# Layer 2's second weight: loaded and converted late, by halves with their own scales, and its output summed in two banks

## The chip, the cores and the metric

The kernel runs on one core of one Trainium2 chip. The metric is device time in microseconds for one execution; shown is the median over runs. Five engines work side by side, each with its own queue that it works through in order: TensorE (PE, matmuls, with its weight loads as PEld), VectorE (DVE), ScalarE (ACT), GpSimd (POOL) and SyncE (SP, which issues the DMAs). In this kernel TensorE's results go to PSUM tiles (three called pb of 1024 fp32 columns, g2_ps and xn_ps of 512); the other tiles lie in SBUF, and two tensors of intermediate results in DRAM.

## The reference

Attention over two sequences of 768 tokens with 8 heads of 64, in which a query sees only the keys whose cluster (the nearest of 16 centroids) is its own; then two feed-forward layers on the 1536 tokens:

```python
x = attn_out.transpose(0, 2, 1, 3).reshape(1536, 512)
h = x @ moe_w_in;   g = h * cos(h);                  x = g @ moe_w_out     # layer 1: 512 -> 2048 -> 512
h = x @ moe2_w_in;  g = h * (1 / (1 + exp(-h)));     out = g @ moe2_w_out  # layer 2: 512 -> 2048 -> 512
```

The four feed-forward weights arrive as fp64 and are read as pairs of 32-bit words, which the kernel puts together into fp32 on the chip ("conversion"); the rest is fp32, and so is the output.

## The kernel before, in words

**Precision.** Each matmul operand is held as two fp16 tiles, a high part and a low part, after multiplication by a power of two, its scale; a product is three matmuls (high x high, high x low, low x high). A scale needs a bound of the whole tensor: the sum of squares of the converted weight, per partition by ScalarE (L438), then over partitions by a small matmul with ones (`all_sum`, L422), then four single-column instructions on VectorE (L443 to L447).

**Order.** The kernel writes down tasks with an engine (sometimes two to choose from), a duration, dependencies, buffers and a priority; a planner (`Graph.run`) simulates them as a list schedule (the ready task with the smallest priority number goes first on its engine) and the instructions are issued in the order that comes out. So each engine's order is fixed in advance by the planner's own durations, and a queue waits where the chip is later than the plan. Work of unit u (128 or 256 tokens) has priority about 1000 x u, layer 2 has `base` = 100000, and the late numbers in `T` shift groups of tasks against each other.

**Stages.** Layer 1's weights are converted first. Seven units of attention follow, each with its scores, softmax, transposes of the probabilities (by DMA, L514) and product with the values (L958); layer 1 of a unit is interleaved with the next unit's attention (L1034 to L1036 into h, L1092 to L1094 out of g). When the last attention task is done, the SBUF tiles of attention are given up and layer 2's are laid in their place (the task `SWAP`).

**Second weight of layer 2, before.** `w2_convert` (L868) has priority 1e6, the last of all, and runs during attention. For each of 16 blocks of 128 x 512 it loads 512 KB of raw words (L692), converts them with VectorE (L704, L706, and L716 in three of four blocks; the fourth has its low word added by ScalarE L710 and GpSimd L711) into half of the tile x2s, takes the squares (L438) and stores 256 KB to DRAM (L875). The swap waits for it. In layer 2 it comes back in 8 loads of 512 KB into two buffers `st` (L1162) and is split (`split`, L752): high part by GpSimd (L754) or ScalarE (L753), rescaling in place by ScalarE (L498), low part by VectorE (L500). Its scale is made to match the two halves of the first weight, so that all 16 blocks of the inner dimension add up in one bank.

**First weight of layer 2.** After the swap, 16 loads into two buffers `ws2`, each converted by VectorE through a PSUM bank (L698, L701, L713), with a scale for each half (inner blocks 0 to 7 and 8 to 15), and split into l2["w"][0] and [1] (L753, L754, L765); the converted fp32 values lie where the second weight's fp16 parts go later, l2["w"][2] and [3].

**Layer 2's passes.** 512 tokens at a time, three times: load x2 from DRAM, maximum over all (L430, L431), scale, split (L1197 ScalarE, L1199 VectorE); 16 blocks of 12 matmuls each into three banks pb (L1217 to L1219), each followed by ScalarE (L1231, L1235) and VectorE (L1233, L1237) that form g; then 4 output blocks of 48 matmuls (L1252 to L1254) into the banks g2_ps and xn_ps in turn, copied out by ScalarE with the factor (L1258) and stored (L1261). "Pass" below is 192 matmuls: an in-pass and an out-pass for each of three groups of tokens, six in all.

Of the kernel before, what the change touches and what calls it, by code (L numbers as in the profile page):

```python
# [22 lines left out]
         PREP=-1178, PREPQ=1263, LD=-4837, LOB=-0.79, WB=-1, HB=1, EB=5, KB=-1.47, GB=1.71, CB=0.8, XB=-0.2, SB=0.71,  # L23
# [229 lines left out]
def mm(n, count):  # L253
    return 0.025 + count * n / 2400.0
# [6 lines left out]
def dma(nbytes):  # L261
    return max(0.18, nbytes / 360e3)
# [9 lines left out]
def fused_kernel(tc, q, k, v, cent, w1i, w1o, w2i, w2o, out, dbg=None):  # L272
# [4 lines left out]
    P = 128  # L277
# [24 lines left out]
    with tc.manual_schedule(), tc.tile_pool(name="dram", bufs=1, space=DRAM) as dpool:  # L302
        x2_dram = dpool.tile([P, ND, B * S], F32, name="x2_dram")
        w2_dram = dpool.tile([P, ND * DF], F32, name="w2_dram")
# [63 lines left out]
        p_x2s, p_w2s = BufPool([x2s[:, :WC]]), BufPool([x2s[:, WC:]])  # L368
# [496 lines left out]
        w2_done = []  # L865
        w2_mx = col(NW)

        def w2_convert():  # L868

            for i in range(NW):  # L870
                fb = Buf(p_w2s)
                pr = 1e6 + i * 10
                t, tq = conv(lambda fb=fb: fb.ap, w2_mx[:, i:i + 1], w2o[i * P:(i + 1) * P, :].bitcast(I32), 0, pr, fb, dst_deps=x_free if 2 in WX else (), add_low=i % 4 < LOW[2], via=i % 4 < VIA[2])
                w2_done.append(tq)
                w2_done.append(add("SP", dma(P * WC * 4), lambda i=i, fb=fb: SP.dma_start(  # L875
                    out=w2_dram[:, i * WC:(i + 1) * WC], in_=fb.ap), [t], pr - 3, use=[fb], lat=SLAT))

# [184 lines left out]
        x2max, x2done = {}, {}  # L1062

        def layer1_out(u):
# [15 lines left out]
            for dp in range(ND // 2):  # L1080
# [28 lines left out]
                te[2 * i:2 * i + 2], pr, use=[x2b[i]], lat=SLAT) for i in range(2)]  # L1109
            x2done[u] = [tmx, *tds]  # L1110
# [5 lines left out]
        def layer2(l1_last):  # L1116
            base = 1e5
            t_swap = add("SWAP", 0.01, lambda: None, [*attn_tasks, *w2_done], 0)
            l2["swap"] = t_swap

            s, inv = [col() for _ in range(3)], [col() for _ in range(3)]
            ready = {}
            mx0 = col(NW)
            p_ws2 = BufPool([0, 1], fifo=False)
            raw = lambda r: l2["w"][:, 2:4].rearrange("p a b -> p (a b)").bitcast(F32)[:, r]
            ms = [[], []]
            for n in range(NW):
                i = (n % 8) // 2 * 4 + n // 8 * 2 + n % 2
                r = slice(i * WC, (i + 1) * WC)
                ms[n // 8] += conv(lambda r=r: raw(r), mx0[:, n:n + 1], w_in_src(w2i, i), 0, base + n * 10 - T["W2"], None, p_ws2, [t_swap], add_low=n % 4 < LOW[3], via=n % 4 < VIA[3])  # L1130
# [206 lines left out]
```

## Time and profile before

| | |
|---|---|
| median of 3 runs | 808.01 us (806.83 to 808.8) |
| profiled execution | 810.0 us, of which the span from first to last instruction 807.2 |
| busy, share of the span | TensorE 711.8 us (88%), VectorE 546.0 (68%), ScalarE 491.0 (61%), GpSimd 287.8 (36%) |
| mean granted TensorE clock | 0.979 of full speed |
| DMA traffic | 111.29 MB, mean 138 GB/s |
| second weight's transfers | 16 of 24 loads of 512 KB (median 4.8 us to landing), 16 stores of 256 KB (2.9), 8 loads of 512 KB (3.9) |

Busy time is a share over stages with different limits: in the attention stage several engines are near their limit, in layer 2 TensorE alone. The profile lists, for each group of instructions of one line, the busy time, the mean of one and the idle time of its engine in front of them with what ended it; waits are put down to the event that came last.

### The profile page before, as it was taken

Reading aid. Unit: us, or ns where it says so; the run is one execution under the profiler, and the core shown is the slowest. Engines: PE = TensorE matmul, PEld = TensorE weight load, DVE = VectorE, ACT = ScalarE, POOL = GpSimd, SP = SyncE. Lnnn points to the kernel's source line nnn. Section 1 sums busy time; section 2 is a strip of 40 time slices with the busy share of each in tenths; the row PEclk is TensorE's granted clock in tenths of the full one; section 3 lists DMA queues with packets and bytes.
Section 4 is the critical chain, followed back from the end, with each engine's and each line's share of the span. In section 5 each row is a group of like instructions: output and inputs, shape, how many; then the busy total and the mean of one; then the engine's idle time right before and its main releaser. Section 6 shows DMA issues by size and latency. Waiting matters only on the chain.

```text
span 807.2 us, 16855 instructions
## 1 busy us (share of the span) xinstructions
PE 711.8 (88%) x6745; PEld 483.9 (60%) x6745; DVE 546.0 (68%) x1156; ACT 491.0 (61%) x769; POOL 287.8 (36%) x240
## 2 busy tenths in 40 slices
PE   2468777988969998998999999998999899999998
PEld 1344344867757876876887888883444344444443
DVE  7899798998987899697688764878850355005400
ACT  4668777798878788698588673756640254014400
POOL 3232467466665457367357531330320000000000
PEclk9999689999998999999999999999999999999999
DMA  8944299989999989959939974432320100000000
GB/s 303 333 158 136 76 211 224 229 146 203 211 185 197 254 155 188 204 127 189 207 108 193 203 229 139 151 119 65 105 66 26 66 1 0 27 27 1 0 27 26
DMA packets 233902, 111.29 MB, mean 138 GB/s; under 512 B 199520, under 2 KB 221536, under 8 KB 233824
## 3 DMA queue, kind: packets, MB, share of 16 engines
q1 hardware_dynamic: 233824, 110.23, 61.4%
q8 instruction: 52, 0.85, 0.5%
q14 instruction: 26, 0.21, 0.1%
HBM read 50.36 MB, written 10.49 MB: 75 GB/s over the span
## 4 chain that ended last, share of the span: by engine, by line
PE 41%; DVE 7%; DMA 4%; ACT 3%; issue 2%; SPq 2%; POOL 1%; ACTq 0%; DVEq 0%; POOLq 0%
PE pb L1219 5%; PE pb L1218 5%; PE pb L1217 5%; DMA gen<-gen 3%; PE xn_ps L1253 3%; PE g_ps L1253 3%; PE xn_ps L1254 3%; PE xn_ps L1252 3%; PE g_ps L1252 3%; PE g_ps L1254 3%; PE g_ps L1094 1%; PE g_ps L1092 1%; PE g_ps L1093 1%; PE pb L1036 1%; PE pb L1035 1%
## 5 line engine op out<-in xcount | busy, mean ns | idle before, releaser
L948 POOL TENSOR_TENSOR gen<-e,gen 128x768 f16<-128x768 f32 x96 | 158.9, 1666 | 58.9 <-ACT gen L941 33.5
L1034 PE MATMUL pb<-xT,w 128*128 128x256 f16 (+1 forms) x448 | 110.9, 261 | 3.6 <-ACT e L934 2.7
L1092 PE MATMUL g_ps<-gT,w 128*128 128x256 f16 (+1 forms) x448 | 110.0, 257 | 1.4 <-ACT x2s L1099 1.4
L934 ACT ACTIVATE e<-pb,small 128x768 f32<-128x768 f32 x96 | 94.6, 990 | 27.2 <-DVE small L919 11.8
L1035 PE MATMUL pb<-xT,w 128*128 128x256 f16 (+1 forms) x448 | 111.1, 261 | 0.0
L1036 PE MATMUL pb<-xT,w 128*128 128x256 f16 (+1 forms) x448 | 110.9, 261 | 0.0
L1093 PE MATMUL g_ps<-gT,w 128*128 128x256 f16 (+1 forms) x448 | 110.0, 257 | 0.2 <-POOL gT L1058 0.2
L1094 PE MATMUL g_ps<-gT,w 128*128 128x256 f16 (+1 forms) x448 | 110.0, 257 | 0.0
L915 DVE TENSOR_REDUCE small<-pb 128x1 f32<-128x768 f32 x96 | 89.7, 950 | 12.6 <-PE pb L905 11.3
L1058 POOL TENSOR_TENSOR gT<-e,gT 128x768 f16<-128x768 f32 (+2 forms) x36 | 56.0, 1560 | 94.0 <-ACT gT L1057 85.9
L905 PE MATMUL pb<-kst,qst 96*128 96x512 f16 (+3 forms) x384 | 79.3, 335 | 10.9 <-ACT e L934 3.6
L958 PE MATMUL xn_ps<-vst,gen 128*128 128x64 f16 x1728 | 66.5, 195 | 20.6 <-DMA gen<-gen 18.9
L958 PEld LDWEIGHTS <-gen 128*128 128x128 f16 x1728 | 60.8, 99 | 33.2 <-DMA gen<-gen 27.0
L1217 PE MATMUL pb<-x2T,w 128*128 128x512 f16 x192 | 73.6, 383 | 5.5 <-DVE w L713 2.0
L1233 DVE SCALAR_TENSOR_TENSOR e<-e,pb 128x512 f32<-128x512 f32 x48 | 32.8, 684 | 62.0 <-ACT e L1231 62.0
L1218 PE MATMUL pb<-x2T,w 128*128 128x512 f16 x192 | 73.4, 382 | 1.0 <-DVE x2T L1199 1.0
L1219 PE MATMUL pb<-x2T,w 128*128 128x512 f16 x192 | 73.5, 383 | 0.0
L941 ACT ACTIVATE gen<-e 128x768 f16<-128x768 f32 x89 | 72.9, 840 | 0.2
L905 PEld LDWEIGHTS <-qst 128*128 128x128 f16 (+1 forms) x384 | 36.0, 100 | 31.9 <-issue 15.5
L1237 DVE SCALAR_TENSOR_TENSOR w<-e,w 128x512 f16<-128x512 f32 x48 | 35.0, 733 | 23.1 <-ACT w L1235 22.9
L1231 ACT ACTIVATE e<-pb,cols 128x512 f32<-128x512 f32 x48 | 32.7, 684 | 28.8 <-PE pb L1219 28.8
L1092 PEld LDWEIGHTS <-w 128*128 128x128 f16 x448 | 43.7, 97 | 9.6 <-issue 1.1
(203 smaller groups left out, 1541.1 us busy)
## 6 DMA issues: line engine op xcount, KB each, us to landing
ws<-in_moe_w_out_dram SPq DMA_DIRECT2D x24, 512.0 KB, 4.8
gT<-in_moe_w_in_dram SPq DMA_DIRECT2D x16, 512.0 KB, 5.0
ws<-in_moe_w_in_dram SPq DMA_DIRECT2D x16, 512.0 KB, 4.4
xT<-in_moe_w_out_dram SPq DMA_DIRECT2D x8, 512.0 KB, 4.5
w_dram<-x2s SPq DMA_DIRECT2D x16, 256.0 KB, 2.9
st<-w_dram SPq DMA_DIRECT2D x8, 512.0 KB, 3.9
stq<-in_q_dram SPq DMA_DIRECT2D x6, 512.0 KB, 5.1
gen<-in_k_dram SPq DMA_DIRECT2D x8, 384.0 KB, 5.0
```

The lines of the kernel that those rows point to most:

```text
L905: PE.matmul(out=sbk.ap[:, c0:c1], lhsT=qs.ap[:kk, a, h], rhs=kb.ap[:kk, a, j].rearrange("p t c -> p (t c)")[:, c0:c1], start=(a == 1), sto ...
L948: tl = add("POOL", pool2(S), lambda hi=hi, lo=lo, ex=ex: PO.tensor_tensor(lo(), ex(), hi(), op=ALU.subtract), [th], pr + T["LO"], use=[*eu ...
L958: PE.matmul(out=o, lhsT=hb.ap[:, pi, kt], rhs=vb.ap[:, vi, j, kt], start=(kt == 0 and pi == 0 and vi == 0), stop=(kt == NT - 1 and pi == 1 ...
L1034: PE.matmul(out=o, lhsT=wh[:, d, fs], rhs=xb.ap[:, 0, d, :n], start=(d == 0), stop=False)
L1035: PE.matmul(out=o, lhsT=wh[:, d, fs], rhs=xb.ap[:, 1, d, :n], start=False, stop=False)
L1036: PE.matmul(out=o, lhsT=wl[:, d, fs], rhs=xb.ap[:, 0, d, :n], start=False, stop=(d == ND - 1))
L1092: PE.matmul(out=o, lhsT=wh, rhs=gh, start=(f == 0 and i == 0), stop=False, skip_group_check=True)
L1093: PE.matmul(out=o, lhsT=wh, rhs=gl, start=False, stop=False, skip_group_check=True)
L1094: PE.matmul(out=o, lhsT=wl, rhs=gh, start=False, stop=(f == NF - 1), skip_group_check=True)
L1217: PE.matmul(out=o, lhsT=wh[:, d, fs], rhs=x[:, 0, d], start=(d == 0), stop=False)
L1218: PE.matmul(out=o, lhsT=wh[:, d, fs], rhs=x[:, 1, d], start=False, stop=False)
L1219: PE.matmul(out=o, lhsT=wl[:, d, fs], rhs=x[:, 0, d], start=False, stop=(d == ND - 1))
```

## The change

The second weight is no longer converted during attention, and its DRAM tile is gone; the swap waits for attention alone. In layer 2, behind the first weight's conversion and through the same pool of load buffers, now four, its 16 blocks are loaded and converted in two halves (inner blocks 0 to 7 and 8 to 15): the first into l2["w"][2] once the first halves of the first weight are split, the second into l2["w"][3] once the second halves are. Each half has its own sum of squares and scale. The first half's fp16 parts go to gT, layer 1's tile, free when layer 1's output is out; the second half's to l2["w"][2]. An output block is formed in two banks, 24 matmuls each: ScalarE copies the first with its factor, VectorE multiplies the second by its own and adds. x2s becomes one pool of two buffers, for layer 1's output too. Two numbers of the planner change: PREPQ (the priority of the queries' preparation) from 1263 to 1889, CB (the handicap of ScalarE against VectorE for a copy of fp16) from 0.8 to 1.16.

```diff
@@ -20,7 +20,7 @@
-         PREP=-1178, PREPQ=1263, LD=-4837, LOB=-0.79, WB=-1, HB=1, EB=5, KB=-1.47, GB=1.71, CB=0.8, XB=-0.2, SB=0.71,
+         PREP=-1178, PREPQ=1889, LD=-4837, LOB=-0.79, WB=-1, HB=1, EB=5, KB=-1.47, GB=1.71, CB=1.16, XB=-0.2, SB=0.71,
...
@@ -365,7 +364,7 @@
-        p_x2s, p_w2s = BufPool([x2s[:, :WC]]), BufPool([x2s[:, WC:]])
+        p_x2s = BufPool([x2s[:, :WC], x2s[:, WC:]])
...
@@ -862,19 +861,6 @@
-        w2_done = []
-        w2_mx = col(NW)
-        def w2_convert():
-            for i in range(NW):
-                fb = Buf(p_w2s)
-                pr = 1e6 + i * 10
-                t, tq = conv(lambda fb=fb: fb.ap, w2_mx[:, i:i + 1], w2o[i * P:(i + 1) * P, :].bitcast(I32), 0, pr, fb, dst_deps=x_free if 2 in WX else (), add_low=i % 4 < LOW[2], via=i % 4 < VIA[2])
-                w2_done.append(tq)
-                w2_done.append(add("SP", dma(P * WC * 4), lambda i=i, fb=fb: SP.dma_start(
-                    out=w2_dram[:, i * WC:(i + 1) * WC], in_=fb.ap), [t], pr - 3, use=[fb], lat=SLAT))
...
@@ -1115,19 +1102,21 @@
-            t_swap = add("SWAP", 0.01, lambda: None, [*attn_tasks, *w2_done], 0)
+            t_swap = add("SWAP", 0.01, lambda: None, attn_tasks, 0)
-            s, inv = [col() for _ in range(3)], [col() for _ in range(3)]
+            s, inv = [col() for _ in range(4)], [col() for _ in range(4)]
-            mx0 = col(NW)
-            p_ws2 = BufPool([0, 1], fifo=False)
-            raw = lambda r: l2["w"][:, 2:4].rearrange("p a b -> p (a b)").bitcast(F32)[:, r]
-            ms = [[], []]
+            mx0, mx1 = col(NW), col(NW)
+            p_ws2 = BufPool([0, 1, 2, 3], fifo=False)
+
+            raw = lambda z, r: l2["w"][:, 2 + z].bitcast(F32)[:, r]
+            ms = [[], [], [], []]
-                r = slice(i * WC, (i + 1) * WC)
-                ms[n // 8] += conv(lambda r=r: raw(r), mx0[:, n:n + 1], w_in_src(w2i, i), 0, base + n * 10 - T["W2"], None, p_ws2, [t_swap], add_low=n % 4 < LOW[3], via=n % 4 < VIA[3])
+                r = slice(n % 8 * WC, (n % 8 + 1) * WC)
+                ms[n // 8] += conv(lambda z=n // 8, r=r: raw(z, r), mx0[:, n:n + 1], w_in_src(w2i, i), 0, base + n * 10 - T["W2"], None, p_ws2, [t_swap],
+                                   add_low=n % 4 < LOW[3], via=n % 4 < VIA[3])
...
@@ -1135,39 +1124,30 @@
                 t, sb_, tot = all_sum(lambda: am[:, 0:1], [t], pr)
                 return add("DVE", 0.66, lambda: wscales(tot(), s[z], inv[z], wk), [t], pr, use=[sb_])
-            t_sc = [f_scale(0, mx0[:, 0:8], ms[0], base), f_scale(1, mx0[:, 8:16], ms[1], base + 50), f_scale(2, w2_mx, w2_done, base)]
+            t_sc = [f_scale(0, mx0[:, 0:8], ms[0], base), f_scale(1, mx0[:, 8:16], ms[1], base + 50)]
             for i in range(ND * DF // 1024):
-                i2 = i % ND * 2 + i // ND
-                r = slice(i2 * 1024, (i2 + 1) * 1024)
-                ready[0, i2] = split(lambda r=r: l2["w"][:, 0, r], lambda r=r: l2["w"][:, 1, r], lambda r=r: raw(r),
-                                     s[i // ND], 1024, [t_sc[i // ND]], base + i + 40 * (i // ND), scale_first=PRE[3][2])
-            so, big, rec, iout = [col(), col()], col(), col(), col()
-            def f_so():
-                DV.tensor_tensor(big, inv[0], inv[1], op=ALU.max)
-                DV.reciprocal(rec, big)
-                for z in range(2):
-                    DV.tensor_scalar(so[z], s[2], inv[z], rec, op0=ALU.mult, op1=ALU.mult)
-                DV.tensor_scalar(iout, inv[2], big, None, op0=ALU.mult)
-            t_so = add("DVE", 0.8, f_so, t_sc, base + 60, port=True)
-            in_done = [ready[0, i] for i in range(ND * DF // 1024)]
-            p_st = [BufPool([i]) for i in range(2)]
-            for i in range(ND * DF // 1024):
-                sbf = Buf(p_st[i % 2])
-                st = lambda sbf=sbf: l2["st"][sbf.ap]
-                r = slice(i * 1024, (i + 1) * 1024)
-                pr = base + 100 + i
-                tl = add("SP", dma(P * 4096), lambda st=st, r=r: SP.dma_start(out=st(), in_=w2_dram[:, r]),
-                         [t_swap], pr, acq=[sbf], lat=LLAT)
-                ready[1, i] = split(lambda r=r: l2["w"][:, 2, r], lambda r=r: l2["w"][:, 3, r], st,
-                                    so[i // 4], 1024, [tl, t_so, *in_done], pr, [sbf], PRE[3][3])
+                z, d = divmod(i, ND)
+                r, ra = slice((2 * d + z) * 1024, (2 * d + z + 1) * 1024), slice(d * 1024, (d + 1) * 1024)
+                ready[0, 2 * d + z] = split(lambda r=r: l2["w"][:, 0, r], lambda r=r: l2["w"][:, 1, r], lambda z=z, ra=ra: raw(z, ra),
+                                            s[z], 1024, [t_sc[z]], base + i + 40 * z, scale_first=PRE[3][2])
+            w2_at = lambda z: l2["w"][:, 2].rearrange("p (a c) -> p a c", a=2) if z else gT.rearrange("p a c -> p (a c)").rearrange("p (a c) -> p a c", a=2)
+            for n in range(NW):
+                z = n // 8
+                r = slice(n % 8 * WC, (n % 8 + 1) * WC)
+                ms[2 + z] += conv(lambda z=z, r=r: raw(z, r), mx1[:, n:n + 1], w2o[n * P:(n + 1) * P, :].bitcast(I32), 0, base + 200 + n * 10, None, p_ws2, [t_swap],
+                                  dst_deps=[ready[0, 2 * d + z] for d in range(ND)], add_low=n % 4 < LOW[2], via=n % 4 < VIA[2])
+            t_sc += [f_scale(2, mx1[:, 0:8], ms[2], base + 290), f_scale(3, mx1[:, 8:16], ms[3], base + 370)]
+            for i in range(8):
+                z = i // 4
+                r = slice(i % 4 * 1024, (i % 4 + 1) * 1024)
+                after = l1_out if z == 0 else [ready[1, j] for j in range(4)]
+                ready[1, i] = split(lambda z=z, r=r: w2_at(z)[:, 0, r], lambda z=z, r=r: w2_at(z)[:, 1, r], lambda z=z, r=r: raw(z, r),
+                                    s[2 + z], 1024, [t_sc[2 + z], *after], base + 300 + 80 * z + i, scale_first=PRE[3][3])
             g2T = w1[:, 0:2]
             p_xf, p_x2 = BufPool([0]), BufPool([0])
             p_g2 = BufPool([0])
             l1_done = l1_last
-            no = 0
             p_ob = [p_g2ps, p_xn]
             for u2 in range(B * S // N2):
                 lo_t, hi_t = u2 * 4, u2 * 4 + 4
...
@@ -1190,7 +1170,9 @@
-                tof = add("DVE", 0.15, lambda ix=ix, ofac=ofac: DV.tensor_scalar(ofac, ix, iout, FG ** -1, op0=ALU.mult, op1=ALU.mult), [ts, t_so], pr)
+                tof = [add("DVE", 0.3, lambda z=z, ix=ix, ofac=ofac: (
+                    DV.tensor_scalar(ofac[z], ix, inv[z], FG ** -1, op0=ALU.mult, op1=ALU.mult),
+                    DV.tensor_scalar(ofac[z], ofac[z], inv[2 + z], None, op0=ALU.mult)), [ts, t_sc[z], t_sc[2 + z]], pr + 290) for z in range(2)]
...
@@ -1238,28 +1220,31 @@
                         g2T[:, 1, sl], rr(), FG / 2, g2T[:, 0, sl], op0=ALU.mult, op1=ALU.subtract), [t], e, use=[rb, gb], port=True)
                     gr.append(t)
                 for t in range(4):
-                    ob = Buf(p_ob[no % 2])
-                    og = Buf((p_x2s, p_w2s)[no % 2])
-                    no += 1
-                    prev = []
-                    for f4 in range(4):
-                        def f_mm(f4=f4, t=t, ob=ob):
-                            wh = l2["w"][:, 2].rearrange("p (f e) -> p f e", e=DM)
-                            wl = l2["w"][:, 3].rearrange("p (f e) -> p f e", e=DM)
-                            for f in range(4 * f4, 4 * f4 + 4):
-                                gh = g2T[:, 0, f * N2 + t * P:f * N2 + (t + 1) * P]
-                                gl = g2T[:, 1, f * N2 + t * P:f * N2 + (t + 1) * P]
-                                PE.matmul(out=ob.ap, lhsT=gh, rhs=wh[:, f], start=(f == 0), stop=False)
-                                PE.matmul(out=ob.ap, lhsT=gh, rhs=wl[:, f], start=False, stop=False)
-                                PE.matmul(out=ob.ap, lhsT=gl, rhs=wh[:, f], start=False, stop=(f == NF - 1))
-
-                        prev = [add("PE", mm(N2, 12), f_mm, [*gr[4 * f4 // step:(4 * f4 + 3) // step + 1], ready[1, 2 * f4], ready[1, 2 * f4 + 1], *prev],
-                                    pr + 300 + t * 10 + f4, acq=[ob], use=[gb])]
-                    to = add("ACT", act(512, SRC), lambda ob=ob, og=og, ofac=ofac: AC.activation(
-                        out=og.ap[:, :DM], in_=ob.ap, func=AF.Copy, scale=ofac), [tof, *prev], pr, acq=[og], use=[ob])
+                    og, to = Buf(p_x2s), None
+                    for z in range(2):
+                        ob, prev = Buf(p_ob[z]), []
+                        for f4 in (2 * z, 2 * z + 1):
+                            def f_mm(f4=f4, z=z, t=t, ob=ob):
+                                wh, wl = (w2_at(z)[:, a].rearrange("p (f e) -> p f e", e=DM) for a in range(2))
+                                for f in range(4 * f4, 4 * f4 + 4):
+                                    gh = g2T[:, 0, f * N2 + t * P:f * N2 + (t + 1) * P]
+                                    gl = g2T[:, 1, f * N2 + t * P:f * N2 + (t + 1) * P]
+                                    w = f - 8 * z
+                                    PE.matmul(out=ob.ap, lhsT=gh, rhs=wh[:, w], start=(w == 0), stop=False)
+                                    PE.matmul(out=ob.ap, lhsT=gh, rhs=wl[:, w], start=False, stop=False)
+                                    PE.matmul(out=ob.ap, lhsT=gl, rhs=wh[:, w], start=False, stop=(w == 7))
+
+                            prev = [add("PE", mm(N2, 12), f_mm, [*gr[4 * f4 // step:(4 * f4 + 3) // step + 1], ready[1, 2 * f4], ready[1, 2 * f4 + 1], *prev],
+                                        pr + 300 + t * 10 + f4, acq=[ob], use=[gb])]
+                        if z == 0:
+                            to = add("ACT", act(512, SRC), lambda ob=ob, og=og, ofac=ofac: AC.activation(
+                                out=og.ap, in_=ob.ap, func=AF.Copy, scale=ofac[0]), [tof[0], *prev], pr, acq=[og], use=[ob])
+                        else:
+                            to = add("DVE", dve(512) + 0.06, lambda ob=ob, og=og, ofac=ofac: DV.scalar_tensor_tensor(
+                                og.ap, ob.ap, ofac[1], og.ap, op0=ALU.mult, op1=ALU.add), [tof[1], to, *prev], pr, use=[ob, og])
                     bb, tt = divmod(lo_t + t, NT)
                     add("SP", dma(P * 2048), lambda og=og, bb=bb, tt=tt: SP.dma_start(
-                        out=out.rearrange("(b p t) e -> b t p e", b=B, t=NT)[bb, tt], in_=og.ap[:, :DM]), [to], pr, use=[og], lat=SLAT)
+                        out=out.rearrange("(b p t) e -> b t p e", b=B, t=NT)[bb, tt], in_=og.ap), [to], pr, use=[og], lat=SLAT)
         firsts = {x[0]: i for i, x in reversed(list(enumerate(UNITS)))}
...
@@ -1297,8 +1280,7 @@
-                l2["ws"] = [sb([P, 2 * WC], I32, f"ws2_{i}", "right") for i in range(2)]
-                l2["st"] = [sb([P, 1024], F32, f"st2_{i}", "right") for i in range(2)]
+                l2["ws"] = [sb([P, 2 * WC], I32, f"ws2_{i}", "right") for i in range(4)]
```

## Rows read from the trace of the kernel before

**Rows 1.** Windows: stage and length, busy us (instructions) by engine, granted clock, DMA share, GB/s.
```profile
145.00:475.00 330.00, 299.07 (x4095) 251.84 (x4093) 272.87 (x586) 263.49 (x430) 186.85 (x125) 0.98 0.99 185
475.00:545.00 70.00, 67.80 (x620) 60.24 (x619) 49.39 (x82) 40.62 (x71) 23.88 (x17) 1.00 0.49 163
545.00:591.00 46.00, 42.10 (x197) 19.01 (x195) 39.02 (x62) 30.69 (x46) 10.30 (x7) 1.00 0.27 80
632.00:641.00 9.00, 5.86 (x21) 2.20 (x19) 5.22 (x22) 3.56 (x4) 0.00 (x0) 0.81 0.32 109
```

**Rows 2.** Timeline of PE in layer 2: start us, us, instruction [idle before <-releaser].
```profile
590.63 0.38 PE L1252 MATMUL g_ps<-w,w 128*128 128x512 f16 x1
...
632.07 0.22 PE L431 MATMUL pb<-dmax,ones 128*128 128x128 bf16 x1
...
636.02 0.38 PE L1218 MATMUL pb<-x2T,w 128*128 128x512 f16 x1 [0.98 <-DVE x2T L1199]
...
641.59 0.38 PE L1218 MATMUL pb<-x2T,w 128*128 128x512 f16 x1
```

**Rows 3.** Groups by form and one line's min/median/max: the second weight's conversion.
```profile
L706 DVE SCALAR_TENSOR_TENSOR x2s<-ws,x2s 128x512 int32<-128x512 int32 x16 | 11.4, 713 | 0.2
L438 ACT ACTIVATE ws<-x2s 128x512 f32<-128x512 f32 x16 | 9.9, 619 | 0.3 <-DVE x2s L716 0.3
L716 DVE SCALAR_TENSOR_TENSOR x2s<-ws,x2s 128x512 int32<-128x512 int32 x12 | 9.7, 805 | 0.1
L704 DVE TENSOR_SCALAR x2s<-ws 128x512 int32<-128x512 int32 x16 | 7.7, 482 | 1.6 <-DMA w_dram<-x2s 1.6
...
L716 DVE SCALAR_TENSOR_TENSOR x2s<-ws,x2s x12: 675/682/2142, 154.7 to 472.8; 128x512 int32<-128x512 int32 x12
```

**Rows 4.** Waits of PE, 145 to 475 us: us in total, times, longest us.
```profile
PE xn_ps L958 <- DMA gen<-gen: 14.9, 18, 1.8
...
PE pb L1034 <- ACT e L934: 2.7, 1, 2.7
...
PE g_ps L1092 <- ACT x2s L1099: 1.0, 2, 0.8
```

**Rows 5.** The chain that ended last, in order of time: start us, us, what.
```profile
336.63 4.54 DMA w_dram<-x2s
...
341.19 0.44 DVE x2s L704
```

**Rows 6.** Waits of SyncE's queue, whole span.
```profile
SPq L875 <- POOL x2s L711: 17.9, 3, 10.0
```

**Rows 7.** Groups by form: the first step of the first weight's conversion.
```profile
L698 DVE TENSOR_SCALAR pb<-ws 128x512 int32<-128x512 int32 x24 | 16.5, 689 | 15.3 <-DMA ws<-in_moe_w_in_dram 13.6 <-ACT e L934 1.5
```

**Rows 8.** Waits of PE, 500 to 650 us.
```profile
PE pb L1217 <- DVE w L713: 2.0, 1, 2.0
PE pb L1217 <- DVE e L1233: 1.9, 1, 1.9
```

**Rows 9.** Groups by form: VectorE, ScalarE and GpSimd in layer 2.
```profile
L1237 DVE SCALAR_TENSOR_TENSOR w<-e,w 128x512 f16<-128x512 f32 x48 | 35.0, 733 | 23.1 <-ACT w L1235 22.9
L1233 DVE SCALAR_TENSOR_TENSOR e<-e,pb 128x512 f32<-128x512 f32 x48 | 32.8, 684 | 62.0 <-ACT e L1231 62.0
...
L765 DVE SCALAR_TENSOR_TENSOR w<-w,cols 128x1024 f16<-128x1024 f32 x11 | 13.8, 1275 | 0.0
L754 POOL TENSOR_SCALAR w<-st,cols 128x1024 f16<-128x1024 f32 x8 | 12.5, 1563 | 27.3 <-DMA st<-w_dram 12.3 <-DVE cols L1151 9.6 <-ACT w L1235 5.3
...
L500 DVE TENSOR_TENSOR w<-st,w 128x1024 f16<-128x1024 f32 x8 | 9.7, 1220 | 3.9 <-ACT st L498 3.9
...
L498 ACT ACTIVATE st<-st,cols 128x1024 f32<-128x1024 f32 x8 | 9.1, 1141 | 3.2 <-POOL w L754 3.1
...
L1199 DVE SCALAR_TENSOR_TENSOR x2T<-xf,cols,x2T 128x1024 f16<-128x1024 f32 x6 | 7.6, 1278 | 0.3 <-ACT x2T L1197 0.3
L447 DVE RECIPROCAL cols<-cols 128x1 f32<-128x1 f32 x30 | 4.9, 163 | 1.0
```

More of the change, by code (lines that the diff above doesn't have):

```diff
@@ L303, in fused_kernel @@
         x2_dram = dpool.tile([P, ND, B * S], F32, name="x2_dram")
-        w2_dram = dpool.tile([P, ND * DF], F32, name="w2_dram")
         pb = [ps([P, 1024], f"pb{i}") for i in range(3)]
@@ L1060, in layer1_in @@
                     alt=("DVE", dve(N4), lambda r=r, sl=sl: DV.tensor_tensor(gb.ap[:, 1, sl], r(), gb.ap[:, 0, sl], op=ALU.subtract), T["GB"]), port=True))
-        x2max, x2done = {}, {}
+        x2max, x2done, l1_out = {}, {}, []
         def layer1_out(u):
@@ L1109, in layer1_out @@
                 te[2 * i:2 * i + 2], pr, use=[x2b[i]], lat=SLAT) for i in range(2)]
+            l1_out.extend(te)
             x2done[u] = [tmx, *tds]
@@ L1178, in layer2 @@
                          [t_swap, *[t for u in us for t in x2done[u][1:]]], pr, acq=[xfb], lat=LLAT)
-                m, am2, sx, ix, ths, ofac, wk2 = col(), col(), col(), col(), [col(), col()], col(), col(3)
+                m, am2, sx, ix, ths, ofac, wk2 = col(), col(), col(), col(), [col(), col()], [col(), col()], col(3)
                 def f_m(us=us, m=m):
@@ L1285, in fused_kernel @@
                 layer1_out(w)
-        G.tag = 'w2c'
-        w2_convert()
         G.tag = 'l2'
```

## The prediction

> **What bounds the kernel now.** I read the windows by stage first [rows 1]. TensorE is busy 299.07 of the 330 us of the attention stage (145 to 475 us), 67.80 of the next 70 (the rest of layer 1), and 42.10 of the 46 in which layer 2 begins. Layer 2 is six passes of 192 matmuls of 512 columns; one pass takes 632.07 - 590.63 = 41.4 us [rows 2], 0.216 us a matmul, and six of them 249 us, which no edit here changes. What can be won or lost is time in which TensorE has nothing to do: 30.9 us in the attention stage, 3.9 us where layer 2 begins, and one hole at 632 us. VectorE stands beside it with 272.87 busy of 330 and, where layer 2 begins, 39.02 of 46.
>
> **Where the removed work sits.** By groups [rows 3], the conversion of the second weight costs VectorE 7.7 + 11.4 + 9.7 = 28.8 us and ScalarE 9.9 us (squares), in the attention stage. It has the planner's last priority, so it mostly fills holes. Of TensorE's waits there the largest, 14.9 us over 18 times, is for the transposes of the probabilities [rows 4], which go through the same SyncE queue and DMA engines as the conversion's 16 loads, 16 stores and 8 loads back. The chain of waits shows the filler on the path once: a store of 4.54 us, then the next conversion's first instruction [rows 5]. And SyncE's queue, which issues in order, stood 17.9 us (3 times) at a store whose data GpSimd had not finished [rows 6].
>
> **The change, term by term.** (1) Attention stage. 28.8 us of VectorE's 272.87 go, 10.6%. If TensorE's holes shrank in proportion, that is 0.106 x 30.9 = 3.3 us; the store on the chain kept VectorE idle for 1.6 us [rows 3], which goes too; together about -5. Bounds: the holes that are not waits for transposes are 30.9 - 14.9 = 16, so at best about -16; at worst +3, because the planner, with the tasks gone and two of its numbers changed (PREPQ, CB), writes a new order over the whole stage, and a single wait of 2.7 us such as L1034's [rows 4] can come anew. I take -5, near the proportional estimate. Two x2s buffers for layer 1's output can save at most the 1.0 us that L1092 waits [rows 4]; I count nothing.
>
> (2) Four buffers for layer 2's weight loads. VectorE waits 13.6 us for the loads of the first weight [rows 7]. TensorE is nearly full then, so by itself that is worth nothing, but the conversion ends earlier, and with it goes the 2.0 us wait of first-pass matmuls on L713, which holds a bank of pb [rows 8]. The next wait, 1.9 us on L1233, comes in the stretch where ScalarE still has squares and may stay with the new squares: I count half. Together -3 (0 to -4).
>
> (3) The second weight's first half. Its conversion can start when the first halves of w_in are split, about where the first pass begins, at 545 us. Half of 28.8 is 14.4 us of VectorE work. Until the pass ends, at 590.6 less the 3 us of (2), VectorE also has 16 blocks of 0.684 + 0.733 us = 22.7 us [rows 9], and four splits and two halves of x2T at 1.28, 7.7 us, partly before 545: 45 in 43, just about in time. But its scale needs a sum over partitions on TensorE at priority base+290, and the first pass's matmuls (base+100 to 180) are always ready: the sum goes behind them. After it come the scale (four single-column instructions of 0.163), then on ScalarE one high part and two rescalings, taken at 1.141 each (GpSimd does the other high part beside them, 1.563), and the low part 1.220 [rows 9]: 0.65 + 3.42 + 1.22, with some 0.7 for the sum and the hand-overs (an estimate) 6.0 us, in which TensorE has nothing. Before, these splits lay beside the first pass, since the scale was known from the attention stage. Then the clock: after the hole at 632 (636.02 - 632.07 = 3.95 us) the granted clock of 632 to 641 is 0.81 in the mean [rows 1]; 18 intervals up to 641.59 took 5.57 us where 18 x 0.216 = 3.88 [rows 2], so 1.7 us were lost. I add the same. Together +7.7; below: 0, if the sum slips in earlier; above: +10, if VectorE is late by some microseconds.
>
> (4) The hole at 632. The next 512 tokens' maximum, scale and split come only after the last output matmul of these, because their small matmul has a later priority: 3.95 us, and 1.7 of slow clock. With TensorE empty at 588 that small matmul runs there, and x2T's split finds its place before the third pass: -5.6. It is 0 if VectorE's more urgent conversions starve the split until the end of the second pass.
>
> (5) The second half. Summing in two banks lets TensorE do the first half of three row blocks (24 matmuls, 5.2 us each; two output buffers and the bank itself hold them) before it needs the second half: until 587.6 + 6.0 + 15.5 = 609. VectorE from 545 on: 22.7 + 28.8 + 8 x 1.22 low parts + 7.7 = 69 us, so 614; another 2 to 4 us for scale and first splits, against 7.8 us of matmuls for the next tokens that can fill (three banks of 12). I take +1 (0 to +14, below).
>
> (6) The end. The last result is now a VectorE sum from PSUM instead of ScalarE's copy; its nearest row (L1233, also from PSUM and of 512 columns) has 0.684, and the copy reads as many columns. 0, between -0.3 and +0.3. Its added wait, for ScalarE's copy of the first half, is over some 4 us earlier (24 matmuls, 5.2 us, lie between), and nothing urgent is queued behind it on VectorE. The sums of all blocks but the last lie beside matmuls.
>
> Sum: -5 - 3 + 7.7 - 5.6 + 1 = -4.9. The profiled execution took 810.0 us (span 807.2), 2 above the median of the runs (808.01), so 805.1 in its terms and 803.1 against the median.
>
> **A rule weighed.** L716 took 0.682 us in the median and 2.142 at the longest; its mean of 0.805 is 1.5 us over 12 instructions [rows 3], some 5 over all 44 if the others fare alike, and the 28.8 above hold that. The Trainium skill (SBUF — State Buffer, Who interferes with whom) says that a VectorE instruction with two inputs in SBUF and a GpSimd instruction that reads SBUF exclude each other for the whole of an instruction. By that rule the conversions, now beside GpSimd's high parts (8 x 1.563 = 12.5 us, rows 9), could lose up to 12.5 us; by the rows 5, with a GpSimd that was busier, and the forecast keeps the rows. What the rule would do is the late-weights rival.
>
> **Rivals.** *Late weights* (slower): VectorE doesn't pack 69 us without holes. At the 39.02 of 46 that it reached in this stage, 85%, 69 us take 81 and the second half comes at 626 plus 3, some 20 us behind 609; less 7.8 of fill it costs about 12. With (1) at -3 and the hole of (4) still saved: -3 - 3 + 7.7 - 5.6 + 12 = +8, 816. It decides from about 6 us of lateness on. For it: VectorE has the least slack exactly here. Against: the 13.6 us of waiting in front of the stage become usable, and a quarter of the conversions have GpSimd's add.
> *All hidden*: a small hole in the first pass lets the sum through, and (3) and (5) are 0: -5 - 3 - 5.6 = -13.6, 794. For it: there were holes of 2.0 and 1.9 in that pass. Against: these are what (2) removes.
> *Filler was free*: the attention stage is paced by TensorE and transposes, (1) is 0, and the other terms cancel: 808. For it: last priority, and one place in the chain. Against: 17.9 us of a stopped queue.
>
> **Chances.** Forecast 0.42 (800 to 806.5), late weights 0.23, all hidden 0.15, free filler 0.20. A measurement here tells about 0.3%, 2.4 us: faster means below 805.6, slower above 810.4. Faster: 0.37 of the forecast, 0.15, 0.03 of free filler = 0.55; slower: 0.20 of late weights and 0.02 = 0.22; the same: 0.23. The range for 8 in 10: 793 (all hidden) to 813 (part of the late weights).
>
> **What would show it.** No w_dram transfer at all; the attention stage's idle TensorE down from 30.9 to about 26; first-weight conversions without waits for loads; a hole of about 6 us before the first output matmul of layer 2, with the sum's matmul at its start and a slow clock behind it; no hole before the third pass. If the first output matmuls start without a hole, (3) is wrong; if TensorE waits over 6 us between the first and the second halves, late weights hold; if attention ends later than 475, (1) has the wrong sign.

## The result and the profile after

The changed kernel took 814.72 us (median of 12 runs, 811.26 to 816.82), the kernel before 808.33 (12 runs beside them, 805.72 to 811.23): ratio 1.0073, 95% interval 1.0052 to 1.0094. It is slower by 0.7%, and outside the range of 793 to 813. Ratios here and below are of undisturbed runs against the kernel before on the same chip, so they need not be the quotient of the medians. The profiled execution took 811.84 us (span 809.7), 2.9 below its median; that of before lay 1.7 above its own. Of the 6 us between the medians the two profiles hold only 2.5 of span.

The windows of the kernel after, the stages of [rows 1] (columns as there), and one more just behind the first pass of layer 2:

```profile
145.00:475.00 330.00, 301.12 (x4090) 253.75 (x4088) 247.85 (x546) 250.97 (x392) 178.58 (x121) 0.97 0.91 154
475.00:545.00 70.00, 67.41 (x619) 60.12 (x617) 55.62 (x90) 43.94 (x77) 22.91 (x17) 1.00 0.50 157
545.00:591.00 46.00, 41.58 (x195) 18.84 (x193) 45.70 (x84) 31.86 (x65) 7.55 (x5) 0.98 0.48 164
591.00:600.00 9.00, 5.40 (x14) 1.88 (x14) 8.96 (x13) 6.36 (x8) 2.73 (x2) 0.53 0.00 1
632.00:641.00 9.00, 9.00 (x44) 4.05 (x43) 0.75 (x1) 0.69 (x1) 0.00 (x0) 1.00 0.01 2
```

VectorE lost 272.87 - 247.85 = 25 us in the attention stage. TensorE is busy 2.05 us longer there, but with 4090 matmuls in place of 4095 and a granted clock of 0.97 in place of 0.98, so that is no work done ahead; in the next stage it is busy 0.39 less. The first pass of layer 2 begins at 545.0 in both profiles. From there VectorE has no room left: 45.70 of 46. The hole at 632 is gone (9.00 of 9 busy, clock 1.00). A new one stands at 586 to 595. The granted clock of 591 to 600 is 0.53, most of it at the lower level of 1.2 GHz.

The waits of TensorE from 545 us to the end (waited for: us, times, longest) give its size:

```profile
PE g_ps L1233 <- POOL gT L753: 5.4, 1, 5.4
PE g_ps L1234 <- DVE gT L499: 2.6, 1, 2.6
PE g_ps L1233 <- ACT x2s L1240: 0.7, 1, 0.7
```

The timeline shows how it comes about, taken from four engines in order of time (start, us, instruction, idle before it):

```profile
577.69 0.14 DVE L1123 TENSOR_REDUCE cols<-cols 128x1 f32<-128x8 f32 x1
...
586.41 0.17 PE L421 MATMUL pb<-cols,ones 128*128 128x1 bf16 x1
...
589.14 0.14 DVE L442 TENSOR_SCALAR cols<-pb 128x1 f32<-128x1 f32 x1
...
590.05 3.67 POOL L753 TENSOR_SCALAR gT<-w,cols 128x1024 f16<-128x1024 f32 x2 [0.29 <-DVE cols L446]
...
590.42 2.17 ACT L752 ACTIVATE gT<-w,cols 128x1024 f16<-128x1024 f32 x2
...
592.00 0.58 PE L1233 MATMUL g_ps<-gT,w 128*128 128x512 f16 x1 [5.43 <-POOL gT L753]
...
592.50 4.25 ACT L497 ACTIVATE w<-w,cols 128x1024 f32<-128x1024 f32 x4
...
593.93 4.61 DVE L499 TENSOR_TENSOR gT<-w,gT 128x1024 f16<-128x1024 f32 x4
...
595.18 0.59 PE L1234 MATMUL g_ps<-gT,w 128*128 128x512 f16 x1 [2.60 <-DVE gT L499]
```

The squares of the first half are summed up at 577.69. The small matmul that sums over partitions (L421) starts 8.7 us later, behind the last matmul of the first pass. The scale (L442) starts another 2.7 us later: VectorE has no idle time, it works off what the planner put in front. Then come GpSimd's high part, which lets the first output matmul start, ScalarE's two high parts and its first rescaling (L497, 1.13 us each, done at 593.6), and the low part (L499) at 593.93, on which the second output matmul waits. Up to 599.40 the matmuls follow each other at 0.427 us in place of 0.216, which costs 2.0 us.

The change did remove what it was to remove before that: VectorE's wait for loads, 13.6 us in [rows 7], is 2.1. But a wait for a sum's matmul, the first weight's, stands beside it now (waits of VectorE, 475 to 545):

```profile
DVE cols L442 <- PE pb L421: 6.8, 1, 6.8
...
DVE pb L697 <- DMA ws<-in_moe_w_in_dram: 2.1, 4, 0.7
```

### The profile page after: what moved, and what is told of

Read it like the earlier page. It is cut to its first block, busy times and chain, and to the rows that moved or that the text cites. A ratio compares the mean times of both kernels' runs of the same rounds, so it can differ in the third digit from the quotient of the medians.

```text
span 809.7 us, 16825 instructions
## 1 busy us (share of the span) xinstructions
PE 712.2 (88%) x6746; PEld 485.9 (60%) x6746; DVE 555.4 (69%) x1181; ACT 492.4 (61%) x769; POOL 277.5 (34%) x235
## 5 line engine op out<-in xcount | busy, mean ns | idle before, releaser
L1044 POOL TENSOR_TENSOR gT<-e,gT 128x768 f16<-128x768 f32 (+2 forms) x36 | 54.3, 1512 | 95.8 <-ACT gT L1043 82.8
L1243 DVE SCALAR_TENSOR_TENSOR x2s<-xn_ps,cols,x2s 128x512 f32<-128x512 f32 x12 | 9.0, 750 | 92.6 <-PE xn_ps L1235 92.6
L927 ACT ACTIVATE gen<-e 128x768 f16<-128x768 f32 x83 | 68.0, 839 | 0.8 <-DMA gen<-gen 0.4
L1240 ACT ACTIVATE x2s<-g_ps,cols 128x512 f32<-128x512 f32 x12 | 8.2, 687 | 85.1 <-PE g_ps L1235 84.4
L1217 ACT ACTIVATE w<-e 128x512 f16<-128x512 f32 x48 | 30.1, 628 | 33.9 <-DVE e L1215 33.9
```

## The experiments

Two theories of the hole. *Position*: it is the way sum, scale, split, which starts only when the first pass has left TensorE. *Capacity*: VectorE has more work between 545 and 592 us than fits. And of the attention stage: that the conversion there delayed TensorE (the forecast), or that it filled holes and cost nothing. "Layer 2 begins" means the first matmul of its first pass.

**The changed kernel again.**

> The changed kernel, unaltered. Its profile put layer 2's start at 545.0 us, where the kernel before also has it, and explains 2.5 us of span, while the medians lie 6.4 apart. Theory A (the loss is the hole of 8 us before the first out-pass with its slow clock, and the attention stage is as long as before): another profile again has layer 2's start within 1.5 us of 545, the hole at 7 to 9 us, and the ratio is 1.004 to 1.010. Theory B (the newly planned attention stage is longer in most executions): layer 2 starts 3 to 5 us later than in the kernel before, and the hole is the same.

Measured 814.0 us (811.76 to 816.39), 1.0047 (1.0024 to 1.0071). In its profile (816.39 us) layer 2 began at 549.1, not 545.0, and the same two waits of 5.5 and 2.6 us follow. So the start of layer 2 differs by 4 us between two executions of one kernel; the hole doesn't. This profile fits theory B and the first one theory A, so the repetition doesn't decide between them.

**The kernel before without the early conversion.**

```
-        w2_convert()
+        PO.memset(w2_mx, 4.0)
...
-  in_=w2_dram[:, r]
+  in_=q (other data, the same bytes)
```

> The kernel before without the conversion of the second weight in the attention stage: no loads, no conversion, no squares, no stores; layer 2 loads q instead of the stored weight through the same eight DMAs, with a constant for the squares. Its output is not the reference's. It prices term 1 by itself. Theory A (the conversion was filler and cost the attention stage nothing): within 2 us of the kernel before, 806 to 810. My forecast's term (5 us gained): 801 to 805. If the planner's new order alone makes the stage longer: above 810.

810.09 us, ratio 1.0007 (0.9984 to 1.003): theory A's time. With 28.8 us of VectorE work and 32 transfers gone the time is the same, so term (1), -5 in the forecast, did not come. That the filler was free is not shown by this alone: without its tasks the planner writes another order for the whole stage. In the profile (815.79 us, the slowest of the ten runs) layer 2 begins at 554.35, 9.4 us later than before, and takes 814.1 - 554.4 = 259.7 us from there, against 262.2 before:

```profile
554.25 0.27 PE L1093 MATMUL g_ps<-gT,w 128*128 128x256 f16 x1
554.35 0.38 PE L1216 MATMUL pb<-x2T,w 128*128 128x512 f16 x1
```

If layer 2 is as short in the other runs, the part before it is about 2.8 us longer at the median (an estimate from these numbers: 2.5 and the 0.3 between the medians).

**The sum of the second weight asked for early.**

```
-  f_scale(2, mx1[:, 0:8], ms[2], base + 290), f_scale(3, mx1[:, 8:16], ms[3], base + 370)
+  f_scale(2, mx1[:, 0:8], ms[2], base + 95), f_scale(3, mx1[:, 8:16], ms[3], base + 370)
```

> The changed kernel with the priority of the sum for the second weight's first half at base+95 instead of base+290, nothing else, so that its small matmul may go before blocks of the first pass that are still to come. If the order is the cause (the sum was ready at 577.7 and went at 586.4), the hole of 8 us falls to under 2 and the kernel gains 7 to 9: 805 to 808. If VectorE is the bound (it had no idle time from 545 to 600), the low parts only push the conversions of the second half back, TensorE waits at the second half instead, and at most 3 us are gained: 811 to 815.

821.08 us (4 runs), 1.0122 (1.009 to 1.0153): slower than the changed kernel by 7, a miss for both theories. In its profile layer 2 begins at 551.3 and takes 269.9 us from there, 5.2 more than in the changed kernel's first profile (264.7). TensorE's waits from 580 us on:

```profile
PE g_ps L1234 <- DVE gT L499: 6.0, 1, 6.0
PE pb L1199 <- ACT x2T L1179: 3.0, 1, 3.0
PE g_ps L1233 <- ACT x2s L1240: 1.8, 1, 1.8
PE pb L1200 <- DVE x2T L1181: 0.9, 1, 0.9
```

The sum did come early: the reciprocal of the scale (584.59, 0.16 us) is done at 584.75 and the first output matmul starts at 593.0 without a wait. Then the low parts are late in VectorE's queue, the second of them at 599.41, and the hole is there again, 6.0 us. The two x2T waits are a second loss: between 720 and 740 us TensorE is busy 16.05 of 20 at a clock of 0.91, where the changed kernel has no hole. One priority is the whole edit; how it leads to that wait was not traced.

**More low words on GpSimd** (the last step of the conversion, not the low part of the split): `LOW = (2,1,4,1)` in place of `(2,1,1,1)`.

> The changed kernel with the low word of all 16 blocks of the second weight added by GpSimd and ScalarE instead of 4 of them: 12 VectorE instructions of 0.68 us (8.2 us) go from VectorE, 12 of about 1.6 come to GpSimd, 12 of 0.68 to ScalarE. The sum stays behind the first pass. If VectorE is the bound: the hole shrinks by 3 to 5 us, 809 to 812. If the order of the sum alone is: the hole stays at 7 to 9, 813 to 816. If GpSimd holds VectorE off the shared port while it adds: VectorE's instructions get longer by several us, 815 or more.

812.49 us, 1.0041 (1.0018 to 1.0064). The waits are 3.2 for the high and 3.2 for the low part, 6.4 in place of 8.0, and 1.6 for L1240. The time lies between the two expected (809 to 812, 813 to 816), its interval overlaps the changed kernel's, and the hole shrank by less than the 3 to 5 us that capacity asked for. Twelve passes of VectorE less don't close the hole, which speaks against capacity alone.

**Without the late conversion**, and without it but with both sums early. The first leaves the sums where the change has them, the second asks for them at base+95 and base+96.

```
-  ms[2 + z] += conv(... w2o[n * P:(n + 1) * P, :] ...)
+  ms[2 + z].append(load of other data into raw(z, r))
```

> Leaves out the conversion of layer 2's second weight: its values are replaced by a plain load of other data into the same place, once the first weight's half has been split off; the sums, the scales, the splits and the two banks stay where the change has them. VectorE loses some 48 instructions (about 30 us) between the layers. Theory 'position' (the hole before the first out-pass is the way of the sum: its matmul stands behind the first in-pass in TensorE's queue, 586.4, then scale, split, 592.0): most of the hole stays, 4 to 6 us in place of 8.0, with its slow clock, and the time is 2 to 4 below the changed kernel's, near 811. Theory 'capacity' (VectorE has more work than fits between 545 and 592, and that alone makes the hole): the hole goes, the clock stays up, and the time is 9 to 11 below the changed kernel's, near 804.

> As the run before (conversion of the second weight left out, other data loaded in its place), and besides with the two sums of the second weight's squares asked for before the first in-pass's work instead of behind it. Both theories, 'position' and 'capacity', say that no hole is left before the first out-pass: 9 to 11 below the changed kernel, near 804. If a hole of over 3 us stays there, both are wrong. A hole of up to 5.6 before the second in-pass, which the kernel before has and the change lost, may come back; then the time is near 809. With this run, the change and the run that only asked for the sums early, the four corners are there: if either cause alone keeps a hole of 5 us and more, the two stand one behind the other.

816.17 us (4 runs, 814.49 to 820.16), 1.01 (1.0062 to 1.0138), and 807.4 us, 0.9985 (0.9961 to 1.0008). The times expected, near 811 and near 804, were both missed; the holes expected by position came. TensorE's waits from 540 us on, of the first and of the second:

```profile
PE g_ps L1235 <- DVE gT L499: 3.9, 1, 3.9
PE pb L1200 <- ACT x2T L1180: 3.0, 1, 3.0
PE g_ps L1234 <- POOL gT L753: 1.7, 1, 1.7
PE pb L1201 <- DVE x2T L1182: 0.7, 1, 0.7
```

```profile
PE pb L1200 <- ACT x2T L1180: 1.6, 1, 1.6
PE pb L1201 <- DVE x2T L1182: 1.6, 1, 1.6
PE pb L430 <- DVE dmax L429: 1.2, 1, 1.2
```

So the four corners of the first output matmuls' waits are: conversion and late sum 8.0; no conversion, late sum 3.9 + 1.7 = 5.6; conversion, early sum 6.0; neither, 0. Each cause alone keeps most of the hole. They stand one behind the other, and each hid what taking the other away was worth. (The fourth corner moves both sums, the third only the first half's.) The first of these kernels is not faster than the changed one; its profile also has a hole at an x2T split between 700 and 760 us (TensorE busy 56.26 of 60 at 0.94); the profile of the second has such a hole at 632, like the kernel before.

**All four sums early, half of the low words on GpSimd.**

```
-LOW = (2,1,1,1)
+LOW = (2,1,2,1)
...
-  t_sc = [f_scale(0, ..., base), f_scale(1, ..., base + 50)]
+  t_sc = [f_scale(0, ..., 1000), f_scale(1, ..., 1000)]
...
-  f_scale(2, ..., base + 290), f_scale(3, ..., base + 370)
+  f_scale(2, ..., base + 95), f_scale(3, ..., base + 96)
```

> The change with all four sums of squares asked for early (the first weight's in place of the layer-1 matmuls' order, so that VectorE does not idle for 6.8 us at 527 to 534 and the second weight's conversion starts sooner) and with half of the second weight's low parts added by GpSimd, as against a quarter. Position: the sum is no longer behind the in-pass, hole 2 or less, time 7 to 9 below the changed kernel's, near 806. Capacity: VectorE gets 6.8 us more before the out-pass and gives away 4 of its passes of 0.70, together 9.6, hole about 0, 10 below the changed kernel's, near 804. Either would be 4 to 5 below the kernel before. If the layer-1 matmuls are delayed by the early sums, as in the sum that was asked for early alone, the gain is lost: 812 and more.

805.99 us (803.61 to 808.56), ratio 0.9961 (0.994 to 0.9982): faster than both, and the time that position had expected. VectorE's wait of 6.8 us is gone, the conversion (L703) starts at 524.3 in place of 552.8, and TensorE's waits from 540 us on are short:

```profile
PE pb L1199 <- DVE e L1215: 1.0, 1, 1.0
PE pb L1200 <- DVE x2T L1181: 0.5, 1, 0.5
PE pb L421 <- DVE cols L1123: 0.3, 1, 0.3
PE g_ps L1233 <- ACT x2s L1240: 0.2, 1, 0.2
```

**The same with the change's own share on GpSimd** (`LOW` as in the change).

> The version with all sums early, but with the quarter of low parts on GpSimd as in the change (not half). Position alone: as that version, 804 to 808, no hole. Capacity behind it: VectorE has 4 passes of 0.70 more, 2.8 us, before the first out-pass, and the hole comes back by 1 to 3 us: 807 to 810.

816.36 us, 1.0061 (1.0031 to 1.0091): both theories, 804 to 808 and 807 to 810, missed the time. The waits on L499 and L753 stay away, as position expected; but waits of 1.4, 1.0 and 1.0 us follow, and the hole at an x2T split comes back (3.0 and 0.7 us, 56.26 busy of 700 to 760 at a clock of 0.94). Four passes of 0.7 us on VectorE decide some 8 us (ratios 1.0061 and 0.9961); in the profiles 7 of them lie behind the first output matmul. With all four sums early the conversion can stay: here too it starts early (L703 at 521.3, against 559.1 where only one sum was early), and there is no hole.

**Four buffers alone**, on the kernel before: the second weight's reload shares them.

```
-  p_ws2 = BufPool([0, 1], fifo=False)
+  p_ws2 = BufPool([0, 1, 2, 3], fifo=False)
...
-  sbf = Buf(p_st[i % 2])
+  sbf = Buf(p_ws2)
```

> The kernel before with one part of the change alone: four load buffers for layer 2's first weight, which the second weight's reload shares, in place of two and two. VectorE's waits for these loads, 13.6 us at 475 to 545, should fall to some 2, and the first in-pass lose its holes of 3.9 us: 3 to 4 below the kernel before, near 805. Rival: the first in-pass waits for something else in their place, and the time is the kernel before's within 0.3 per cent.

808.12 us, 0.9976 (0.9949 to 1.0004): the interval reaches 1, and the 3 to 4 us expected are not shown in the time. In its profile the waits for loads are 2.3 us, the first pass has no holes, and from the first pass to the end it is 805.7 - 547.6 = 258.1 us, against 807.2 - 545.0 = 262.2 before: -4.1, as expected for this part. The start of layer 2, 547.6 in that execution, takes 2.6 of it back.

**Two banks alone**, on the kernel before.

```
-  f4 in range(4), one ob, one AC.activation(..., scale=ofac)
+  for z in range(2): f4 in (2z, 2z+1), ob of its own;
+    z = 0: AC.activation, z = 1: DV.scalar_tensor_tensor(og, ob, ofac, og)
```

> The kernel before with one part of the change alone: each output row block summed in two banks of 24 matmuls, ScalarE copying the first with the scale and VectorE adding the second, in place of one sum of 48 and one copy. 16 scalar_tensor_tensor of 0.75 us come to VectorE, all but the last beside the matmuls. Forecast's view: 0 to +0.5, same as the kernel before. Rival: the last copy, the add and the store stand behind the last matmul, +0.7 at most; or the bank freed later keeps matmuls waiting, +2 and more.

812.14 us, 1.001 (0.9981 to 1.0039): no difference. The last sum of VectorE starts at 804.64 of a span of 808.5 (3.9 to the end), where ScalarE's last copy before started 3.7 before the end.

**The conversion left in attention beside the late one**, with PREPQ and CB as before, and **PREPQ and CB alone**: these two kernels differ only in the filler and what it needs: half of x2s, and a swap that waits for it.

```
+  w2_convert()   (first kernel; loaded, converted, stored, not used)
...
-  PREPQ=1889 ... CB=1.16
+  PREPQ=1263 ... CB=0.8   (both)
```

> The change with the early conversion of the second weight left in beside the late one (loaded, converted and written to DRAM in the attention stage as in the kernel before, and then not used), and with the two planner numbers PREPQ and CB of the kernel before: the attention stage is the one before, all of layer 2 is the changed one. It tells whether taking the filler work out of attention earned or cost anything. Forecast's view (the conversion on VectorE delayed attention by 5): 5 above the changed kernel, near 820. Free filler: the same as the changed kernel within 2, 813 to 816. Filler gone costs a little (the medians of the changed kernel and of the run without any conversion put the start of layer 2 some 2 to 3 us later than the kernel before): 2 to 4 below the changed kernel, near 811.

> The change with only the two planner numbers PREPQ and CB of the kernel before (1263 and 0.8 in place of 1889 and 1.16), which place the later query preparations and weigh VectorE against ScalarE for the copies. If the numbers were chosen to fit the lighter attention stage, it is 1 to 3 above the changed kernel, near 816. If they make the start of layer 2 later, it is 2 below, near 812. If they do nothing, within 1.

811.86 us, 1.0007 (0.9976 to 1.0038), and 817.33 us, 1.0094 (1.0062 to 1.0126). Taking the filler out of the attention stage cost 5.5 us between the medians, and the intervals lie apart; the forecast had +5 for leaving it in. The second is 2.6 above the changed kernel's first median, as expected if the two numbers fit the lighter stage, but the intervals overlap. The windows from 475 to 545 us and TensorE's first waits in layer 2, of the kernel with filler and then of the one without:

```profile
475.00:545.00 70.00, 67.66 (x619) 60.13 (x617) 56.72 (x92) 43.64 (x77) 24.00 (x18) 1.00 0.60 194
...
PE g_ps L1248 <- POOL gT L754: 2.8, 1, 2.8
PE g_ps L1249 <- DVE gT L500: 2.4, 1, 2.4
```

```profile
475.00:545.00 70.00, 67.24 (x618) 60.04 (x616) 53.43 (x89) 45.76 (x79) 24.29 (x18) 1.00 0.52 171
...
PE g_ps L1233 <- POOL gT L753: 5.4, 1, 5.4
PE g_ps L1234 <- DVE gT L499: 2.6, 1, 2.6
```

With the filler VectorE is busy 3.3 us more in this window; five of the first weight's eight low parts start in it, against two without. The hole is 5.2 us in place of 8.0. The kernel without the filler has the wait of 6.8 us for L421 that the changed kernel has; in the one with it the longest single wait of VectorE there is 2.3. Layer 2 also begins at 545.3 with it and at 548.0 without, which may be the spread between executions.

## Why the prediction was wrong

Two terms account for most of it: the gain in the attention stage, (1), which did not come, and the hole before the first output matmuls, (3), which was sized 3 us too small. Point by point, by its terms:

(1) *Attention stage, forecast -5, measured 0 or worse.* This is the step that failed. TensorE's idle time was to fall in proportion to VectorE's work, to about 26 us; it is 28.9, at a slightly lower clock, the first pass starts at 545.0 in both profiles, and the kernel before without the conversion is no faster. With and without the filler beside the late conversion, the kernel without it is the slower one by 5.5 us. The rival "filler was free" was nearest on this point, though its time, 808, was not met. That a store stood once on the chain [rows 5] and that SyncE's queue had stood for 17.9 us [rows 6] put no price on the work: the longest wait of TensorE was for the transposes [rows 4] and did not go with it (14.9 us before; 10.3 in this profile and 15.9 in the repeated run's, 145 to 475 us). Beyond that the order written without the filler puts the first weight's sums behind layer 1's matmuls, the 6.8 us in which VectorE idles ahead of its fullest stretch. "Some wait can come anew" was in the bounds, up to +3.

(2) *Four buffers, forecast -3.* -3.9 in the profile (no hole in the first pass), and -4.1 from the first pass on with that part alone.

(3) *The hole before the first output matmuls, forecast +7.7.* The mechanism was right: the sum stands behind the first pass, and the clock falls. The size was 5.4 + 2.6 = 8.0 and 2.0 of slow clock, and 0.7 more on L1240: 10.7, just above the bound of +10. What was left out is VectorE's queue in front of the scale, 2.7 us: "just about in time" (45 us in 43) was taken as no delay. From the scale to the second output matmul it is 595.18 - 589.14 = 6.0 us (with one matmul in it), about what the forecast had for the whole way, 6.0.

(4) *The hole at 632, forecast -5.6.* It went. In four of the experiments a hole of this kind came back, in three at a later pass and in one at 632, so the gain belongs to this order and not to the late load.

(5) *The second half, forecast +1.* No wait shows for it. The late-weights rival asked for over 6 us between the first and the second halves, so that its 816 lies near the measured time is luck. The conversion took 11.7 + 8.5 + 7.0 = 27.2 us of VectorE, less than the 28.8 of [rows 3]. The exclusion of VectorE and GpSimd that the Trainium skill describes (SBUF — State Buffer, Who interferes with whom) shows in this trace, at far less than the 12.5 us weighed: between 545 and 615 us four VectorE instructions are slowed, each beside a GpSimd instruction, by 2.3 us together. Some of them, and their usual times:

```profile
577.05 1.85 POOL L710 TENSOR_TENSOR w<-w,ws 128x512 int32<-128x512 int32 x1 [10.21 <-ACT w L1217]
578.35 1.11 DVE L705 SCALAR_TENSOR_TENSOR w<-ws,w 128x512 int32<-128x512 int32 x1
...
581.19 0.75 DVE L703 TENSOR_SCALAR w<-ws 128x512 int32<-128x512 int32 x2
581.86 0.68 DVE L705 SCALAR_TENSOR_TENSOR w<-ws,w 128x512 int32<-128x512 int32 x1
...
592.41 1.59 DVE L703 TENSOR_SCALAR w<-ws 128x512 int32<-128x512 int32 x2
```

Beside GpSimd's add, L705 takes 1.11 us in place of 0.68; beside its high parts (590.05 to 593.72), the pair of L703 takes 1.59 in place of 0.75, right in front of the first low part. There it delays little: the rescaling is done only at 593.6, and the low part starts at 593.93.

(6) *The end, forecast 0.* No measurable difference from two banks alone.

In the profiles: 0 - 3.9 + 10.7 - 5.65 + 0.5 (the last sum to the end, 4.2 against 3.7) = +1.7, of 2.5 seen. From its start to the end layer 2 takes 264.7 and 265.6 us in the two profiles of the changed kernel, against 262.2 before, which is 2.5 to 3.4 of the 6.4 and 4.2 us between the medians. The remaining 1 to 4 us lie before layer 2, by subtraction. With one profile for each kernel (two of the changed one), layer 2 begins at 545.0, 547.6, 544.8 and 545.3 where the early conversion is kept, and at 545.0, 549.1, 551.3, 545.4, 544.8, 545.3, 548.0 and 554.4 where it is not (leaving out the two kernels whose first pass starts among layer 1's matmuls): 2.2 later in the mean, with a scatter larger than that. The pair with and without filler points the same way, at the order written for the lighter stage. Which wait in the attention stage makes it stays open, and that PREPQ and CB as changed win some of it back (817.33 with the old ones) is not shown.

## What to carry to other kernels

Work of last priority that fits in holes may cost nothing where it is: here taking it out of the attention stage gained nothing, in two pairs of kernels. Moved to a later, full stage it can take the path, and the first thing to ask there is not only its volume but which small step it makes urgent: here a reduction of one column whose matmul stood 8.7 us behind the rest of a pass. Where a wait has two causes in a row, taking one away shows little (8.0 us became 5.6 or 6.0, and 0 without both): test both corners before a cause is dismissed.

## What the runs showed beside that

After a hole of 8.0 us the matmuls ran at 0.427 us each up to 599.40 and then at 0.216 at once; 2.0 us were lost. After the 3.95 us before [rows 2] the first matmuls still came at 0.216, the slow ones from 636.88 to 640.25; 1.7 us were lost. After the 6.0 us with the sum asked for early, the matmuls were slow from 600.68 to 605.75, and 2.5 us were lost. So the loss did not follow the length of the hole (the one of 8.0 has a single matmul in it, after 5.4). And two executions of the changed kernel differ by 4.1 us in when layer 2 begins, where its twelve runs span 5.6.
